# The last 64 rows of two weight matrices on low partitions, and q computed in rows, in a gated attention and MLP decode kernel

## The chip, the cores and the metric

One core of one Trainium2 chip runs the kernel. The metric is the device time of one execution in microseconds (us). Engines are named as the profile names them: PE (matrix multiply), PEld (its weight loads), DVE (vector), ACT (scalar), POOL (GpSimd), SP (the engine that issues most transfers). "SPq" and "ACTq" are the instruction streams that issue transfers. Sixteen DMA engines serve the core; a transfer issued by one instruction is split over some or all of them.

## What is computed

```python
x: [8, 1, 448]                                 # B = 8 rows, D = 448
g = sigmoid((x * gate_w).sum(-1))
# attention, 16 query heads on 8 key/value heads, the last 1024 of 4096 cached positions
q = x @ wq                                     # wq [448, 4096]
p = softmax(q . k / 16) ; o = p . v            # k, v [8, 8, 1024, 256] of the caches
a = o @ wo                                     # wo [4096, 448]
# MLP
h = gelu(layernorm(x) @ w1 + b1)               # w1 [448, 1792]
b = h @ w2 + b2                                # w2 [1792, 448]
out = g * a + (1 - g) * b
```

All inputs are bf16. Keys and values are 33.6 MB each; with the weights some 77.7 MB are read for an output of 8 x 448 numbers.

## The kernel before

**Weights and inputs.** D = 448 is 3 x 128 + 64. The first 384 rows of wq and w1 lie in `wq_sb` and `w1_sb` on 128 partitions, three rows to a partition. The last 64 rows are the tail. Before the change each tail row is cut in two halves, so that the tail also fills 128 partitions: `wq_t` [128, 2048] and `w1_t` [128, 896]. The matching parts of x and of the normalised y are spread over 128 columns with zeros between (`x_e`, `y_e`, `halves`, L263), turned by PE (L273) and copied to `xT` and `yT` (L276).

**Order of the transfers.** ACT issues x, b1 and b2 (L156 to L158). SP issues w1_sb (L159), w1_t (L162), w2 (L164), three parts of wq_sb (L167) and wq_t (L168). Then `issue_to` (L187, L148) goes through a fixed list: 32 key tiles and 32 value tiles of 1 MB, with a 448 KB part of wo (`wo_sb[g]`) after every fourth key tile; the value tile lags the key tile by five; the last value tile comes in two halves, and the last wo part is the last transfer of all. Keys and values share a pool of 12 buffers (`NKV`), and a load into a used buffer waits until PE has read it. Transfers of SP and ACT together take turns on eight completion semaphores; a transfer waits until the one that used its semaphore before has landed. So at most eight are under way.

**Start of the computation.** `mlp_up` makes 14 groups of matmuls: three with `w1_sb` (L321), one with b1 (L325), one with `w1_t` (L329). DVE and ACT do the gelu (L338 to L344). `mlp_down` (L353) multiplies with w2 on two column strips of PE, 28 matmuls of 224 columns and two for b2. Then q: 128 matmuls with a 128 x 128 block of wq as the weights and 8 columns of xT (L377), which gives q already turned; two DVE instructions scale it into `qT` (L389).

**The long loop.** There are 64 steps. A step turns half a key tile with 16 PE transposes (L407), copies the result out of PSUM (DVE, L412), multiplies the step before with qT (scores, L433) and, eleven steps later, the value half tile with the softmaxed scores (`pv`, L508). Every eight steps a head's softmax is done and its part of the output projection (`o_proj`, L533). `gate_load` and `gate` are done in the middle. PE, DVE and SP take everything in program order.

**The end.** After the last value half: `pv`, `o_scale` on DVE (L519), `o_proj` with the last wo part (L533), one DVE instruction (L577), two output transfers (L581).

Of the kernel before, what the change touches and what calls it, by code (L numbers as in the profile page):

```python
# [16 lines left out]
def kernel(  # L17
# [15 lines left out]
    nc = tc.nc  # L33
# [10 lines left out]
    NB = B  # L44
# [8 lines left out]
    DC = D // P  # L53
    DM = DC * P
    TL = D - DM
    HH = HD // 2
    assert Sq == 1 and Dh % P == 0 and W % P == 0 and F % P == 0
    FH = F // 2
    NH = NF // 2
    assert TL * 2 == P and NC * R <= 2 * P and NB % TB == 0 and 3 * 32 <= P and R <= 32 and NF % 2 == 0  # L60
    qscale = float(Dh) ** -0.5
    NU = NBU * Hkv
    NSTEP = NU * TB
# [42 lines left out]
    big.tile([P, PAD], BF16, name="pad")  # L106
    NKH = rep * NJ
    wq_sb = big.tile([P, DC, HD], BF16, name="wq_sb")
    wq_t = big.tile([P, HH], BF16, name="wq_t")
    w1_sb = big.tile([P, DC, F], BF16, name="w1_sb")  # L110
    wo_sb = [big.tile([P, NKH, D], BF16, name=f"wo_sb{g}") for g in range(Hkv)]
    w1_t = big.tile([P, FH], BF16, name="w1_t")
    w2_sb = big.tile([P, NF, D], BF16, name="w2_sb")
    x_sb = consts.tile([NB, D], BF16, name="x_sb")
    gw_sb = consts.tile([NB, D], BF16, name="gw_sb")
    b1_sb = consts.tile([1, F], BF16, name="b1_sb")
# [10 lines left out]
    xT = consts.tile([P, DC + 2, NB], BF16, name="xT")  # L127
    yT = consts.tile([P, DC + 2, NB], BF16, name="yT")
    x_e = consts.tile([NB, 2, P], BF16, name="x_e")
    y_e = consts.tile([NB, 2, P], BF16, name="y_e")  # L130
    gg = consts.tile([NB, 2], F32, name="gg")
    gg4 = consts.tile([PT, 2], F32, name="gg4")
    bvec = consts.tile([PT, DN], F32, name="bvec")
    bsum = consts.tile([PT, DN], F32, name="bsum")
    res = consts.tile([PT, DN], BF16, name="res")

# [4 lines left out]
    def load(kind, n):  # L141
# [40 lines left out]
    def issue_to(k):  # L182
        while pos[0] < len(units):
            kind, n = units[pos[0]]
            if kind == "W":
                r0 = n * NKH * P
                nc.sync.dma_start(  # L187
                    wo_sb[n][:].rearrange("p (i j) n -> p i (j n)", i=rep),
                    A_wo[r0 : r0 + NKH * P, :].rearrange(
                        "(i p j) n -> p i (j n)", i=rep, j=NJ  # L190
                    ),
                )
# [26 lines left out]
    )  # L219
    for t in diag:  # L220
        nc.gpsimd.memset(t[:], 0.0)
    nc.gpsimd.memset(x_e[:], 0.0)
    nc.gpsimd.memset(y_e[:], 0.0)
    nc.gpsimd.tensor_copy(identf[:], ident[:])
    sel = consts.tile([NB, PT], F32, name="sel")
    nc.gpsimd.tensor_copy(
        sel[:].rearrange("b (j q) -> b j q", j=CT),
        ident[0:NB, 0:CP].unsqueeze(1).to_broadcast([NB, CT, CP]),
    )


    prod = consts.tile([NB, D], F32, name="prod")
# [28 lines left out]
    def halves(dst, src):
        for h in range(2):
            nc.vector.tensor_copy(  # L263
                dst[:, h, :].rearrange("b (r h) -> b r h", h=2)[:, :, h],
                src[:, DM:D],
            )

    def transposed(dst, t, t_e):
        v = t[:, 0:DM].rearrange("b (p c) -> b c p", c=DC)
        parts = [v[:, c, :] for c in range(DC)] + [t_e[:, h, :] for h in range(2)]  # L270
        tp = ps_kt.tile([P, W], BF16, tag="ktp", name="tp")
        for c, part in enumerate(parts):
            nc.tensor.transpose(  # L273
                tp[:, c * NB : (c + 1) * NB], part, ident[0:NB, 0:NB]
            )
        nc.vector.tensor_copy(  # L276
            dst[:], tp[:, 0 : len(parts) * NB].rearrange("p (c b) -> p c b", b=NB)
        )

    halves(y_e, y_sb)  # L280
    transposed(yT, y_sb, y_e)
    halves(x_e, x_sb)
    transposed(xT, x_sb, x_e)


    def gate_load():
        src = gate_w.rearrange("(o d) -> o d", o=1)
        nc.scalar.dma_start(gw_sb[:], src.to_broadcast([NB, D]))

    def gate():  # L290
        nc.vector.tensor_tensor(prod[:], x_sb[:], gw_sb[:], op=ALU.mult)
# [13 lines left out]
        nc.vector.tensor_copy(gg4[:], A_bank[0:PT, DN : DN + 2])  # L305
        nc.vector.tensor_scalar_mul(bvec[:], bsum[:], gg4[:, 1:2])


    M = {}
# [58 lines left out]
    q_ps = ps_g.tile([P, 512], F32, tag="grp", name="q_ps")
    NQ = Hq * NJ
    for c in range(DC + 1):  # L370
        for k in range(NQ):
            if c < DC:
                w, xs = wq_sb[:, c, k * P : (k + 1) * P], xT[:, c, :]
            else:
                h, kk = divmod(k, NQ // 2)
                w, xs = wq_t[:, kk * P : (kk + 1) * P], xT[:, DC + h, :]
            nc.tensor.matmul(  # L377
                q_ps[:, k * NB : (k + 1) * NB],
                lhsT=w,
                rhs=xs,  # L380
                start=(c == 0 and k == 0),
                stop=(c == DC),
                skip_group_check=True,
            )
# [161 lines left out]
    for n in range(LAST):  # L546
# [65 lines left out]
```

## Time and profile before

| what | value |
|---|---|
| median of 3 runs | 196.84 us (196.69 to 196.88) |
| the profiled execution | 196.92 us |
| its span in the profile | 195.2 us, so 1.72 us lie outside |
| PE busy, DVE busy, ACT busy | 164.2, 113.1, 6.4 us |
| DMA read | 77.68 MB, 398 GB/s over the span |
| last wo part landed | 191.33 us |
| mean granted PE clock | 0.768 |

The page gives busy times by engine, a row of 40 slices, the DMA queues, the chain of work that ended last, and the costliest groups of instructions. The trace behind it also holds one record for each DMA packet (start, duration, bytes, queue) and one for each increment that a DMA engine made on a completion semaphore. A transfer on 16 DMA engines makes 16 such increments, one as each engine's share has landed. Queue q1 is that of SP, q10 that of ACT; q8 and q14 fetch instructions for the engines.

### The profile page before, as it was taken

To read this page: it belongs to the slowest core of one execution; us is meant where nothing else is said; L and a number is where in the kernel's file an instruction comes from. 1 tells how busy PE (TensorE), PEld (TensorE's weight loads), DVE (VectorE), ACT (ScalarE), POOL (GpSimd) and SP (SyncE) were. 2 spreads that over 40 slices of the span, in tenths; PEclk is the share of its full clock that TensorE was granted. 3 is DMA by queue.
4 is the path that set the end of the run, shared out by engine and by line. 5 is a ranking of instruction groups with operands and counts; after the bars stand their busy time and mean duration, and the time that the engine had idled before them with its cause. 6 is when DMAs were issued, how large, how long until landed. Compare 5 with 4: busy or idle time off the path is not lost.

```text
span 195.2 us, 7355 instructions
## 1 busy us (share of the span) xinstructions
PE 164.2 (84%) x3417; PEld 153.6 (79%) x3417; DVE 113.1 (58%) x255; ACT 6.4 (3%) x13; POOL 2.8 (1%) x16
## 2 busy tenths in 40 slices
PE   2677799988899796958999898988898989989752
PEld 1565799988899796957999797978897989989541
DVE  3122189996477653764559674964586646766401
ACT  5000000000000000010000000000000000000000
POOL 5000000000000000000000000000000000000000
PEclk9999889997569855585569996995599655699555
DMA  6999999999999999999999999999999999999940
GB/s 215 412 426 425 425 413 426 426 423 420 421 426 422 417 425 426 425 417 431 423 423 419 422 425 428 418 421 418 425 430 417 421 425 430 426 420 425 394 176 5
DMA packets 12769, 78.14 MB, mean 400 GB/s; under 512 B 1330, under 2 KB 3523, under 8 KB 4164
## 3 DMA queue, kind: packets, MB, share of 16 engines
q1 hardware_dynamic: 12688, 77.67, 95.4%
q8 instruction: 26, 0.43, 0.8%
q10 hardware_dynamic: 52, 0.02, 0.0%
q14 instruction: 3, 0.02, 0.0%
HBM read 77.68 MB, written 0.01 MB: 398 GB/s over the span
## 4 chain that ended last, share of the span: by engine, by line
DMA 91%; PE 6%; SPq 1%; issue 0%; DVE 0%
DMA kv<-in_A_k_cache_dram 47%; DMA kv<-in_A_v_cache_dram 19%; DMA wo_sb<-in_A_wo_dram 18%; DMA wq_sb<-in_A_wq_dram 7%; PE ktp L407 4%; PE grp L433 1%; PE A_bank L533 0%; PE grp L508 0%; SPq L167 0%; PE grp L422 0%; SPq L164 0%; DVE res L577 0%; SPq L159 0%; SPq L162 0%; SPq L148 0%
## 5 line engine op out<-in xcount | busy, mean ns | idle before, releaser
L412 DVE COPY kt<-ktp 128x1024 bf16<-128x1024 bf16 x128 | 84.4, 687 | 44.4 <-PE ktp L407 43.9
L407 PE MATMUL ktp<-ident,kv 128*128 128x128 bf16 x1024 | 89.0, 257 | 7.9 <-DMA kv<-in_A_k_cache_dram 6.7
L407 PEld LDWEIGHTS <-kv 128*128 128x128 bf16 x1024 | 78.0, 118 | 10.9 <-DMA kv<-in_A_k_cache_dram 7.9
L508 PE MATMUL grp<-e,kv 128*128 128x4 bf16 x1024 | 35.6, 166 | 2.6 <-DMA kv<-in_A_v_cache_dram 2.5
L508 PEld LDWEIGHTS <-kv 128*128 128x128 bf16 x1024 | 32.6, 101 | 5.6 <-DMA kv<-in_A_v_cache_dram 2.8
L433 PE MATMUL grp<-qT,kt 128*128 128x4 bf16 x1024 | 36.6, 166 | 0.3 <-DVE kt L412 0.2
L433 PEld LDWEIGHTS <-kt 128*128 128x128 bf16 x1024 | 34.6, 100 | 1.8 <-issue 0.6
L482 ACT ACTIVATE e<-grp 128x256 bf16<-128x256 f32 x8 | 3.1, 383 | 161.8 <-PE grp L475 161.8
L491 PE MATMUL A_bank<-zs,onesf 128*128 128x16 f32 x16 | 3.6, 299 | 4.5 <-DVE zs L487 4.5
L491 PEld LDWEIGHTS A_bank<-zs,onesf 128*128 128x128 f32 x16 | 2.8, 218 | 5.1 <-DVE zs L487 5.1
L533 PE MATMUL A_bank<-wo_sb,ot 128*8 128x224 bf16 x64 | 5.5, 305 | 0.8 <-DMA wo_sb<-in_A_wo_dram 0.5
L321 PE MATMUL h_ps<-yT,w_sb 128*128 128x8 bf16 x42 | 4.2, 195 | 1.2 <-DMA w_sb<-in_B_w_dram 1.2
L495 DVE RECIPROCAL rz<-A_bank 128x16 f32<-128x16 f32 x8 | 2.1, 258 | 5.4 <-PE A_bank L491 5.4
L519 DVE TENSOR_TENSOR ot<-grp,rz 128x32 bf16<-128x32 f32 x8 | 1.5, 186 | 6.4 <-PE grp L508 6.4
L487 DVE TENSOR_REDUCE zs<-e 128x16 f32<-128x256 bf16 x8 | 4.8, 602 | 0.0
L353 PE MATMUL b_ps<-w_sb,hT 128*8 128x224 bf16 x28 | 2.8, 388 | 2.4 <-DVE b_ps L349 2.4
L338 DVE COPY z<-h_ps 128x112 f32<-128x112 f32 x1 | 0.3, 275 | 7.7 <-PE h_ps L329 7.7
L321 PEld LDWEIGHTS <-w_sb 128*128 128x128 bf16 x42 | 3.6, 152 | 1.3 <-DMA w_sb<-in_B_w_dram 1.3
L475 PE MATMUL grp<-diag,onesb 128*128 128x256 bf16 x8 | 2.5, 308 | 2.2 <-DVE diag L469 1.9
L353 PEld LDWEIGHTS <-hT 128*8 128x8 bf16 x28 | 1.8, 121 | 3.0 <-DVE hT L344 2.2
L446 DVE TENSOR_REDUCE pm<-grp 128x16 f32<-128x256 f32 x8 | 3.3, 415 | 0.6 <-PE grp L433 0.6
L533 PEld LDWEIGHTS <-ot 128*8 128x8 bf16 x64 | 2.6, 93 | 1.3 <-issue 0.4
(82 smaller groups left out, 53.6 us busy)
## 6 DMA issues: line engine op xcount, KB each, us to landing
kv<-in_A_k_cache_dram SPq DMA_DIRECT2D x32, 1024.0 KB, 18.3
kv<-in_A_v_cache_dram SPq DMA_DIRECT2D x31, 1024.0 KB, 18.3
wo_sb<-in_A_wo_dram SPq DMA_DIRECT2D x8, 448.0 KB, 18.3
wq_sb<-in_A_wq_dram SPq DMA_DIRECT2D x3, 1024.0 KB, 12.1
w_sb<-in_B_w_dram SPq DMA_DIRECT2D x1, 1568.0 KB
w_sb<-in_B_w_dram SPq DMA_DIRECT2D x1, 1344.0 KB, 5.9
kv<-in_A_v_cache_dram SPq DMA_DIRECT2D x2, 512.0 KB, 19.8
wq_t<-in_A_wq_dram SPq DMA_DIRECT2D x1, 512.0 KB, 14.5
```

Source lines behind the costliest of these rows:

```text
L321: nc.tensor.matmul(o, lhsT=cols(w1_sb[:, c, h * FH : (h + 1) * FH]), rhs=yT[:, c, :], start=(c == 0), stop=False,)
L353: nc.tensor.matmul(b_ps[CP * j : CP * j + NB, 0:DN], lhsT=M["hT"][:, k * NB : (k + 1) * NB] if k < NF else onesb[0:1, 0:NB], rhs=w2_sb[:, ...
L407: nc.tensor.transpose(ktp[:, c * P : (c + 1) * P], K[:, h * HC + c, j * P : (j + 1) * P], ident[:],)
L412: nc.vector.tensor_copy(kt[:, j, :], ktp[:])
L433: nc.tensor.matmul(G[g][:, s : s + RU], lhsT=kt[:, j, c * P : (c + 1) * P], rhs=qT[:, j, g, bu * TB : (bu + 1) * TB, :].rearrange("p t i - ...
L446: nc.vector.reduce_max(pm[:], G[g][:, S0 : S0 + NC * R].rearrange("p (c r) -> p r c", r=R), axis=AXIS.X,)
L475: nc.tensor.matmul(G[g][:, S0 : S0 + NC * R].rearrange("p (c r) -> p c r", c=NC), lhsT=onesb[:], rhs=diag[g % 2][:].unsqueeze(1).to_broadc ...
L482: nc.scalar.activation(e[:], G[g][:, S0 : S0 + NC * R], ACT.Exp)
L487: nc.vector.reduce_sum(zs[:], E[g][:].rearrange("p (c r) -> p r c", r=R), axis=AXIS.X)
L491: nc.tensor.matmul(zc, lhsT=onesf[:], rhs=zs[:], start=False, stop=True, skip_group_check=True)
L508: nc.tensor.matmul(G[g][:, o : o + RU], lhsT=V[:, cc, :].rearrange("p (q j) -> p j q", j=NJ)[:, j, :], rhs=E[g][:, cc * R + bu * RU : cc * ...
L533: nc.tensor.matmul(A_bank[CP * j : CP * j + NB, 0:DN], lhsT=ot[:].rearrange("p j (b i) -> p j i b", i=rep)[:, h, i, :], rhs=wo_sb[g][:, k, ...
```

## The change

Four things change together.

1. **The tails.** The tail rows are no longer cut in two. Rows 0 to 47 of the tail go to partitions 0 to 23 and 32 to 55 of `wq_t` and `w1_t` by two transfers whose source has the outer dimension 6 (six groups of four rows); rows 48 to 63 go to partitions 0 to 15 of `wq_u` and `w1_u` by one transfer of outer dimension 4. A row is 8192 B for wq and 3584 B for w1. `wq_u` and `w1_u` lie in the memory of the last four wo parts. The unused partitions of `wq_t` and `w1_t` are set to zero first, by POOL and DVE. The three transfers of w1 are issued by ACT and those of wq by SP, after the POOL work; all key, value and wo loads are issued behind them.
2. **b1** is loaded as row 64 of `w1_t`, and row 64 of that part of `yT` is set to 1, so one matmul of 65 rows takes the place of the b1 matmul. The small tail part is one more matmul; there are still five in a group.
3. **q** is computed with 32 columns of xT as the weights (8 of them used) and 512 columns of wq streaming: 5 x 8 matmuls on four column strips, into two PSUM banks. DVE and ACT scale one bank each into `q_r`, PE turns it with 8 transposes, DVE makes qT of it with four copies.
4. **Memory.** gw_sb lies in w1_sb, and bvec in bsum.

On the instruction streams PE goes from 6801 to 6641 rows; SP has three transfers for the wq tail and none for the w1 tail; ACT has the three w1 transfers ahead of its first activation.

```diff
-    wq_t = big.tile([P, HH], BF16, name="wq_t")
+    wq_t = big.tile([P, HD], BF16, name="wq_t")
...
+    NHI = 4
+    wo_sb = [big.tile([P, NKH, D], BF16, name=f"wo_sb{g}") for g in range(Hkv - NHI)]
+    wo_hi = big.tile([P, NHI * NKH * D], BF16, name="wo_hi")
...
+    wq_u = wo_hi[0:T2, 0:HD]
+    w1_u = wo_hi[0:T2, HD : HD + F]
+    w1_t = big.tile([P, F], BF16, name="w1_t")
...
+    def tail(eng, dst1, dst2, w):
+        for h in range(2):
+            eng.dma_start(
+                dst1[32 * h : 32 * h + T1 // 2, :],
+                w[DM + h * T1 // 2 : DM + (h + 1) * T1 // 2, :].rearrange(
+                    "(r i) n -> i r n", i=6
+                ),
+            )
+        eng.dma_start(dst2, w[DM + T1 : D, :].rearrange("(r i) n -> i r n", i=4))
+
+    nc.vector.memset(w1_t[0:TP, :], 0.0)
     nc.scalar.dma_start(x_sb[:], xf)
-    nc.scalar.dma_start(b1_sb[:], B_b1.rearrange("(o f) -> o f", o=1))
+    nc.scalar.dma_start(w1_t[TP : TP + 1, :], B_b1.rearrange("(o f) -> o f", o=1))
...
-    nc.sync.dma_start(w1_t[:], B_w1[DM:D, :].rearrange("r (h n) -> (r h) n", h=2))
+    tail(nc.scalar, w1_t, w1_u, B_w1)
...
-    nc.sync.dma_start(wq_t[:], A_wq[DM:D, :].rearrange("r (h n) -> (r h) n", h=2))
...
-    issue_to(NKV)
...
+    nc.gpsimd.memset(wq_t[0:TP, :], 0.0)
+    tail(nc.sync, wq_t, wq_u, A_wq)
+    issue_to(NKV)
...
-                nc.tensor.matmul(
-                    o, lhsT=cols(b1_sb[:, h * FH : (h + 1) * FH]),
-                    rhs=onesb[0:1, 0:NB], start=False, stop=False,
-                )
-                nc.tensor.matmul(
-                    o, lhsT=cols(w1_t[:]), rhs=yT[:, DC + h, :],
-                    start=False, stop=True,
-                )
+                nc.tensor.matmul(
+                    o, lhsT=cols(w1_t[0 : TP + 1, h * FH : (h + 1) * FH]),
+                    rhs=yT[0 : TP + 1, DC, 0:NB], start=False, stop=False,
+                )
+                nc.tensor.matmul(
+                    o, lhsT=cols(w1_u[:, h * FH : (h + 1) * FH]),
+                    rhs=yT[0:T2, DC + 1, 0:NB], start=False, stop=True,
+                )
...
+    q_ps = [ps_g.tile([P, QW], F32, tag="grp", name="q_ps") for _ in range(NT)]
+    wq_c = [(wq_sb[:, c, :], xT[:, c, :]) for c in range(DC)]
+    wq_c += [(wq_t[0:TP, :], xT[0:TP, DC, :]), (wq_u, xT[0:T2, DC + 1, :])]
+    for c, (w, xs) in enumerate(wq_c):
+        for t in range(NT):
+            for k in range(NS):
+                n0 = QW * (NS * t + k)
+                nc.tensor.matmul(
+                    q_ps[t][CP * k : CP * (k + 1), :],
+                    lhsT=xs,
+                    rhs=w[:, n0 : n0 + QW],
+                    start=(c == 0),
+                    stop=(c == len(wq_c) - 1),
+                    tile_position=(0, CP * k),
+                    skip_group_check=True,
+                )
+    nc.vector.tensor_scalar_mul(q_r[:, 0:QW], q_ps[0][:], qscale)
+    nc.scalar.activation(q_r[:, QW : 2 * QW], q_ps[1][:], ACT.Copy, scale=qscale)
+    for t in range(NT):
+        for k in range(rep * NJ):
+            o = (t * rep * NJ + k) * P
+            nc.tensor.transpose(q_tp[:, o : o + P], q_r[:, o : o + P], ident[:])
+    for t in range(NT):
+        for i in range(rep):
+            nc.vector.tensor_copy(
+                qT[:, :, NS * t : NS * (t + 1), :, i], q_v[:, t, i, :, :, 0:NB]
+            )
```

More of the change, by code (lines that the diff above doesn't have):

```diff
@@ L55 @@
     TL = D - DM
-    HH = HD // 2
+    T1, T2, TP = 48, 16, 64
     assert Sq == 1 and Dh % P == 0 and W % P == 0 and F % P == 0
@@ L59 @@
     NH = NF // 2
-    assert TL * 2 == P and NC * R <= 2 * P and NB % TB == 0 and 3 * 32 <= P and R <= 32 and NF % 2 == 0
+    assert TL == T1 + T2 and F % P == 0 and NC * R <= 2 * P and NB % TB == 0 and 3 * 32 <= P and R <= 32 and NF % 2 == 0
     qscale = float(Dh) ** -0.5
@@ L108 @@
     wq_sb = big.tile([P, DC, HD], BF16, name="wq_sb")
-    wq_t = big.tile([P, HH], BF16, name="wq_t")
+    wq_t = big.tile([P, HD], BF16, name="wq_t")
     w1_sb = big.tile([P, DC, F], BF16, name="w1_sb")
-    wo_sb = [big.tile([P, NKH, D], BF16, name=f"wo_sb{g}") for g in range(Hkv)]
-    w1_t = big.tile([P, FH], BF16, name="w1_t")
+    NHI = 4
+    wo_sb = [big.tile([P, NKH, D], BF16, name=f"wo_sb{g}") for g in range(Hkv - NHI)]
+    wo_hi = big.tile([P, NHI * NKH * D], BF16, name="wo_hi")
+    wo_sb += [
+        wo_hi[:, k * NKH * D : (k + 1) * NKH * D].rearrange("p (k n) -> p k n", n=D)
+        for k in range(NHI)
+    ]
+    wq_u = wo_hi[0:T2, 0:HD]
+    w1_u = wo_hi[0:T2, HD : HD + F]
+    assert HD + F <= NHI * NKH * D
+    w1_t = big.tile([P, F], BF16, name="w1_t")
     w2_sb = big.tile([P, NF, D], BF16, name="w2_sb")
     x_sb = consts.tile([NB, D], BF16, name="x_sb")
-    gw_sb = consts.tile([NB, D], BF16, name="gw_sb")
-    b1_sb = consts.tile([1, F], BF16, name="b1_sb")
+    gw_sb = w1_sb[0:NB, 0, 0:D]
     b2_sb = consts.tile([1, D], BF16, name="b2_sb")
@@ L126 @@
     qT = consts.tile([P, NJ, Hkv, NB, rep], BF16, name="qT")
[L127 to L130, printed above, removed]
+    xT = consts.tile([P, DC + 2, CP], BF16, name="xT")
+    yT = consts.tile([P, DC + 2, CP], BF16, name="yT")
+    x_e = consts.tile([NB, TP + T2], BF16, name="x_e")
+    y_e = consts.tile([NB, TP + T2], BF16, name="y_e")
     gg = consts.tile([NB, 2], F32, name="gg")
     gg4 = consts.tile([PT, 2], F32, name="gg4")
-    bvec = consts.tile([PT, DN], F32, name="bvec")
     bsum = consts.tile([PT, DN], F32, name="bsum")
@@ L187, in issue_to @@
                 nc.sync.dma_start(
-                    wo_sb[n][:].rearrange("p (i j) n -> p i (j n)", i=rep),
+                    wo_sb[n][:, :, :].rearrange("p (i j) n -> p i (j n)", i=rep),
                     A_wo[r0 : r0 + NKH * P, :].rearrange(
@@ L221 @@
         nc.gpsimd.memset(t[:], 0.0)
-    nc.gpsimd.memset(x_e[:], 0.0)
-    nc.gpsimd.memset(y_e[:], 0.0)
+    for t in (x_e, y_e, xT, yT):
+        nc.gpsimd.memset(t[:], 0.0)
+    nc.gpsimd.memset(yT[TP : TP + 1, DC, :], 1.0)
     nc.gpsimd.tensor_copy(identf[:], ident[:])
@@ L259, with transposed @@
     )
[L261 to L265, printed above, removed]
-            )
[L268 to L272, printed above, removed]
+    def transposed(dst, t, t_e):
+        nc.vector.tensor_copy(
+            t_e[:, 0:TP].rearrange("b (h z) -> b h z", h=2)[:, :, 0 : T1 // 2].rearrange(
+                "b h (i r) -> b h i r", r=4
+            ),
+            t[:, DM : DM + T1].rearrange("b (h r i) -> b h i r", h=2, i=6),
+        )
+        nc.vector.tensor_copy(
+            t_e[:, TP : TP + T2].rearrange("b (i r) -> b i r", r=4),
+            t[:, DM + T1 : D].rearrange("b (r i) -> b i r", i=4),
+        )
+        v = t[:, 0:DM].rearrange("b (p c) -> b c p", c=DC)
+        tp = ps_kt.tile([P, W], BF16, tag="ktp", name="tp")
+        for c in range(DC):
+            nc.tensor.transpose(
+                tp[:, c * NB : (c + 1) * NB], v[:, c, :], ident[0:NB, 0:NB]
+            )
+        for c, (lo, n) in enumerate(((0, TP), (TP, T2))):
             nc.tensor.transpose(
-                tp[:, c * NB : (c + 1) * NB], part, ident[0:NB, 0:NB]
+                tp[0:n, (DC + c) * NB : (DC + c + 1) * NB],
+                t_e[:, lo : lo + n], ident[0:NB, 0:NB],
             )
         nc.vector.tensor_copy(
-            dst[:], tp[:, 0 : len(parts) * NB].rearrange("p (c b) -> p c b", b=NB)
+            dst[:, 0:DC, 0:NB], tp[:, 0 : DC * NB].rearrange("p (c b) -> p c b", b=NB)
         )
-    halves(y_e, y_sb)
+        for c, n in enumerate((TP, T2)):
+            nc.vector.tensor_copy(
+                dst[0:n, DC + c, 0:NB], tp[0:n, (DC + c) * NB : (DC + c + 1) * NB]
+            )
     transposed(yT, y_sb, y_e)
-    halves(x_e, x_sb)
     transposed(xT, x_sb, x_e)
@@ L287, in gate_load @@
         src = gate_w.rearrange("(o d) -> o d", o=1)
-        nc.scalar.dma_start(gw_sb[:], src.to_broadcast([NB, D]))
+        nc.scalar.dma_start(gw_sb, src.to_broadcast([NB, D]))
     def gate():
-        nc.vector.tensor_tensor(prod[:], x_sb[:], gw_sb[:], op=ALU.mult)
+        nc.vector.tensor_tensor(prod[:], x_sb[:], gw_sb, op=ALU.mult)
         nc.vector.reduce_sum(gsum[:], prod[:], axis=AXIS.X)
@@ L305, in gate @@
         nc.vector.tensor_copy(gg4[:], A_bank[0:PT, DN : DN + 2])
-        nc.vector.tensor_scalar_mul(bvec[:], bsum[:], gg4[:, 1:2])
+        nc.vector.tensor_scalar_mul(bsum[:], bsum[:], gg4[:, 1:2])
     M = {}
@@ L322, in mlp_up @@
                         o, lhsT=cols(w1_sb[:, c, h * FH : (h + 1) * FH]),
-                        rhs=yT[:, c, :], start=(c == 0), stop=False,
+                        rhs=yT[:, c, 0:NB], start=(c == 0), stop=False,
                     )
                 nc.tensor.matmul(
-                    o, lhsT=cols(b1_sb[:, h * FH : (h + 1) * FH]),
-                    rhs=onesb[0:1, 0:NB], start=False, stop=False,
+                    o, lhsT=cols(w1_t[0 : TP + 1, h * FH : (h + 1) * FH]),
+                    rhs=yT[0 : TP + 1, DC, 0:NB], start=False, stop=False,
                 )
                 nc.tensor.matmul(
-                    o, lhsT=cols(w1_t[:]), rhs=yT[:, DC + h, :],
-                    start=False, stop=True,
+                    o, lhsT=cols(w1_u[:, h * FH : (h + 1) * FH]),
+                    rhs=yT[0:T2, DC + 1, 0:NB], start=False, stop=True,
                 )
@@ L365 @@
     mlp_down()
[L368 to L376, printed above, removed]
-            nc.tensor.matmul(
[L378 to L383, printed above, removed]
-            )
@@ L385 @@
-    q_v = q_ps[:, 0 : Hq * NJ * NB].rearrange(
-        "p (g i j b) -> p i j g b", i=rep, j=NJ, b=NB
-    )
-    for i in range(rep):
-        nc.vector.tensor_scalar_mul(qT[:, :, :, :, i], q_v[:, i], qscale)
+    QW = 512
+    NS = P // CP
+    NT = HD // (NS * QW)
+    assert QW == rep * NJ * P and NT * NS == Hkv
+    q_ps = [ps_g.tile([P, QW], F32, tag="grp", name="q_ps") for _ in range(NT)]
+    wq_c = [(wq_sb[:, c, :], xT[:, c, :]) for c in range(DC)]
+    wq_c += [(wq_t[0:TP, :], xT[0:TP, DC, :]), (wq_u, xT[0:T2, DC + 1, :])]
@@ new lines @@
+    q_r = ktpool.tile([P, NJ, W], BF16, tag="kt", name="q_r")
+    q_r = q_r[:].rearrange("p j w -> p (j w)")
+    nc.vector.tensor_scalar_mul(q_r[:, 0:QW], q_ps[0][:], qscale)
+    nc.scalar.activation(q_r[:, QW : 2 * QW], q_ps[1][:], ACT.Copy, scale=qscale)
+    q_tp = ps_kt.tile([P, W], BF16, tag="ktp", name="q_tp")
+    for t in range(NT):
+        for k in range(rep * NJ):
+            o = (t * rep * NJ + k) * P
+            nc.tensor.transpose(q_tp[:, o : o + P], q_r[:, o : o + P], ident[:])
@@ L392 @@
+    q_v = q_tp[:].rearrange(
+        "p (t i j s z) -> p t i j s z", t=NT, i=rep, j=NJ, s=NS
+    )
+    for t in range(NT):
+        for i in range(rep):
+            nc.vector.tensor_copy(
+                qT[:, :, NS * t : NS * (t + 1), :, i], q_v[:, t, i, :, :, 0:NB]
+            )
     KT = {}
@@ L577 @@
     nc.vector.scalar_tensor_tensor(
-        res[:], in0=A_ps, scalar=gg4[:, 0:1], in1=bvec[:], op0=ALU.mult, op1=ALU.add
+        res[:], in0=A_ps, scalar=gg4[:, 0:1], in1=bsum[:], op0=ALU.mult, op1=ALU.add
     )
```

## The prediction, made before the changed kernel had run

> **What bounds the kernel now.** I read the slices first, then the queues, then the chain of work that ended last, and last the packet and landing records of the trace.
>
> ```profile
> PE   2677799988899796958999898988898989989752
> PEclk9999889997569855585569996995599655699555
> DMA  6999999999999999999999999999999999999940
> ...
> q1 hardware_dynamic: 12688, 77.67, 95.4%
> q8 instruction: 26, 0.43, 0.8%
> ...
> DMA 91%; PE 6%; SPq 1%; issue 0%; DVE 0%
> ```
>
> The DMA engines are full from the second slice to the 38th. PE is busy, but its granted clock falls to half in many slices and its work still gets done: it follows the loads. The chain says the same; its last pieces (start, length, what) are:
>
> ```profile
> 154.50 19.52 DMA kv<-in_A_k_cache_dram
> 174.01 0.02 issue
> 174.03 17.30 DMA wo_sb<-in_A_wo_dram
> 191.33 0.04 issue
> 191.37 0.93 PE A_bank L533 x8
> ```
>
> The last wo part was issued at 174.03 and landed at 191.33; 3.87 us later the span ends. So the end is set by the landing of the last transfer. But the DMA row falls to 4 in the slice from 185.4, five microseconds before that landing. Why? The trace has one landing per DMA engine. For the last transfer, counted from the first at 184.98 us:
>
> ```
> 0  .07  .14  .43  .49  .52  .73  1.88 | 4.65  4.71  4.72  4.74  4.80  4.91  5.67  6.35
> ```
>
> For the third part of wq_sb, at 17.48 us, the sixteen lay within 0.86. So **eight engines fall behind by over 4 us, and the kernel waits for the slowest one**. The packet records show why: each of the 26 fetches on q8 (16 KB, 0.88 to 0.97 us) lengthens the next 8 KB packet of that engine from 0.31 to about 0.8, together 1.43 us. After each fetch exactly one engine's landings jump by that much, and the jumps go round eight engines; the first of them has been hit four times by the 25th fetch (180.7) and is the 6.35. The other eight are never hit by q8. The 1.88 is an engine on which two 8 KB fetches of q14 (at 40.95 and 123.95) cost 0.84 each.
>
> **The step that matters: where the tails go.** A packet of 8192 B takes 306 ns from start to start on its engine, 4096 B 155, 1792 B 71; a row of 3584 B (b1's packet) 137. Before, each engine had 8 packets of 4096 B (wq_t) and 8 of 1792 B (w1_t): 8 x 0.155 + 8 x 0.071 = 1.81 us.
>
> In the trace a transfer has as many landings as its outer dimension allows: x and gate_w (8 rows) eight, b1 (one row) one, all others 16. So I take outer dimension 6 as six engines with four rows each, and 4 as four. If each begins at the same first engine:
> - four engines get 12 rows of each tail: 12 x 0.306 + 12 x 0.137 = 5.31, that is +3.50 us;
> - two get 8 rows: 8 x 0.306 + 8 x 0.137 = 3.54, +1.73 us;
> - ten get none: -1.81 us.
>
> Which engines are these? Packets on one engine follow each other in a fixed rhythm, so each can be followed by its phase, and q10's packets show as steps in it. gate_w's eight packets (63.3 to 63.6 us) fell on six engines that q8 never hits and on two that it hits. b1's single packet (5.09 us) was on one of the six. So the set of one lies in the set of eight, and I take the sets of four and six to nest likewise; that the six are just the never-hit ones is my choice, since the two hit ones follow each other in the round and a run of eight neighbours that leaves out the first engine would have them at the end of the eight. The trace doesn't number the engines.
>
> At the last transfer these six had 0, .07, .14, .48, about .5, and 1.88. Sum at the end: the slowest engine 6.35 - 1.81 = **4.54**; the other hit ones at most 5.67 - 1.81 = 3.86; the four at most .52 + 3.50 = 4.02; the 1.88 engine 1.88 + 1.73 = 3.61 if it is among the two, 5.38 if among the four. I take the first (b1's engine is a different one, and a uniform pick would make it 2 in 5; but if a queue's fetches go to neighbours, as I take q8's to, it is as likely in either pair; I call it four to three). The last landing moves from 191.33 to 189.52: **-1.81 us**. The profiled execution, 196.92, becomes 195.11; its median stood 0.08 below it.
>
> The Trainium skill, "DMA: Bandwidth & Descriptors", speaks against this change in "Rules for kernel authors": a small outermost dimension confines a transfer to few engines, so put a multiple of 16 there. Its section "Why a DMA increments its semaphore by 16 and not by 1" says that SP's and ACT's transfers use the lowest-numbered engines, which agrees with the nesting above. By the rule alone the four engines' 3.50 us would all be added, giving 200.4; by the landings they have 4.1 us of slack and nothing is added.
>
> **What lies beside it.**
> - The start of PE's work gets later, under cover. The w1 tail is on q10 beside q1. b1, issued at 1.43, landed at 5.96; 12 packets that alternate with w2's (235 ns) add up to 12 x (0.137 + 0.235) = 4.5. So L329's successor starts between 7 and 10.6 us instead of 7.3. ACT issues three transfers (0.23 to 0.59 each) after a DVE memset (about 1 us; 224 columns took 0.24) ahead of rstd, so yT comes 1 to 2.5 us later, inside that. Queued behind are the gelu on DVE and ACT, mlp_down, q.
> - q: 40 matmuls of 512 columns. Nearest row:
>
> ```profile
> L353 PE MATMUL b_ps<-w_sb,hT 128*8 128x224 bf16 x28 | 2.8, 388 | 2.4 <-DVE b_ps L349 2.4
> ```
>
> 28 of 224 columns on two strips in 2.78 us, 0.099 each, or 0.44 ns a column: the strips did not overlap. 40 x 512 x 0.44 = 9.0 us against 3.5 (18.73 to 22.2) now: +5.5; were four strips side by side, a quarter, 2.3: -1.2. I take 9.0, the nearer row. (The skill's "TensorEngine Tiling (Array Packing)", "Theoretical Speedup", allows up to 4 times for 32 columns, which would be the 2.3; L353 shows none of it for two.) Scaling and turning add some 1.5 (16 transposes take 1.05; a DVE instruction of 224 columns 0.38). So the first key transposes start between 23 and 34 us, now 23.54. Key tile 0 itself lands at about 25, behind the tails on the four engines.
> - What hides this: 12 buffers, and a queue in which a load waits 18 us.
>
> ```profile
> SPq L148 <- PE ktp L407: 4.4, 12, 0.6
> ```
>
> SP has waited for PE to free a buffer for 0.6 us at most, with 18.3 us of transfers queued ahead. Ten microseconds of lateness halve that queue and leave the engines fed. PE then catches up: a step with pv takes 1.7 us at full clock, two steps 3.4, while a key and a value tile take 4.9. Without this cover each microsecond beyond 18 would stall the loads.
> - SP's three wq-tail transfers wait for POOL's memset (256 columns took 0.30, so 4096 some 3 to 5 us, done by about 9), and SP's next transfers for the eight semaphores, w2's landing among them (near 12). By then wq_sb is queued to 17: hidden; if not, the same price.
> - PE has 160 rows fewer of 6801, that is 0.6 of a fetch (262 rows each): the 25th moves from 180.7 to about 184, still before its engine ends. Should it miss, the four engines' 4.02 would set the end: 194.6.
> - Memory reuse (gw_sb, bsum, wo_hi) waits only for work long done: nothing.
>
> **At the end** PE must not become late:
>
> ```profile
> 187.79 1.01 PE L508 MATMUL grp<-e,kv 128*128 128x4 bf16 x32 [1.41 <-DMA kv<-in_A_v_cache_dram]
> 189.01 0.59 PE L508 MATMUL grp<-e,kv 128*128 128x4 bf16 x16 [0.20 <-DMA kv<-in_A_v_cache_dram]
> 190.24 0.58 PE L508 MATMUL grp<-e,kv 128*128 128x4 bf16 x16 [0.64 <-DMA kv<-in_A_v_cache_dram]
> ```
>
> PE waited 1.41 + 0.20 + 0.64 = 2.25 us here for values. With values 1.81 earlier, 0.44 is left even if PE's own schedule doesn't move.
>
> **Rivals.**
> 1. The 1.88 engine is one of the four: 5.38 sets the end, -0.97: 195.9. For it: nothing numbers the engine. Against: only the pairing above.
> 2. One of the four is an engine that q8 hits: 4.65 to 4.91 before, plus 3.50, is 8.2 to 8.4, +1.8 to +2.1: **198.9, slower**. It decides as soon as one of the four was more than 6.35 - 3.50 = 2.85 behind; among the two, a hit one gives 4.65 + 1.73 = 6.4, no change. Against it: b1's engine is not hit, and six of the eight aren't.
> 3. PE is late at the end by more than the 0.44, because it caught up badly after the late start or ran its last part at half clock as it does now (0.50 after 180): the gain shrinks from 1.81 towards nothing, 195.5 to 196.8.
> 4. The change doesn't do what it says: the shares are spread evenly over all 16 (6 + 6 + 4) or begin elsewhere each time. Then all engines carry about what they did, and the time stays at 196.8.
>
> **Numbers.** Forecast (with a missed fetch) 40%, rival 1 30%, rival 3 10% (a third of it no change), rival 4 6%, rival 2 and anything like it 14%. What a measurement can tell from no change is about 0.2%, 0.4 us. Faster: 40 + 30 + 7 = 77%; same 6 + 3 = 9%; slower 14%. Range: 194.4 (missed fetch, with 0.2 to spare) to 196.9, which takes in all but rival 2; the forecast's own range is 194.6 to 195.6.
>
> **What would show it.** The landings of the last transfer should span some 4.5 us instead of 6.35, the last near 189.5; the wq tail should have 6, 6 and 4 landings. Key tile 0 should land near 25, PE's first key transposes start near 30. Wrong would be a span of landings of 8 with four engines last (rival 2), a wait of PE for nothing but itself after 185 (rival 3), or SP's waits for PE growing to many microseconds.

## The result, and the profile after

The changed kernel takes **197.81 us** (median of 6 executions, 197.10 to 198.66), the kernel before 196.84 (196.64 to 197.00, 6 executions on the same chip). The ratio is 1.0049, with a 95% interval of 1.0031 to 1.0067: it is slower by half a per cent, where 195.1 was forecast. The six executions are not one cluster: 197.10, 197.11, 197.52, 198.09, 198.54, 198.66. The profiled one took 197.11, its span is 195.4.

The page of the changed kernel, in the rows that were read before (slices, then queues with packets, MB and share, then the shares of the chain that ended last):

```profile
PEclk9999999999975556985558969997985555996655
DMA  6999999999999999999999999999999999999940
...
q1 hardware_dynamic: 12480, 77.44, 95.0%
q8 instruction: 26, 0.43, 0.8%
q10 hardware_dynamic: 132, 0.25, 0.4%
...
DMA 81%; PE 13%; POOL 3%; DVE 1%; issue 0%; POOLq 0%; SPq 0%
```

Nothing has changed in kind: the DMA row is full to slice 38 and then falls to 4, as before, and q8 still makes 26 fetches. The last pieces of the chain (start, length, what):

```profile
156.04 19.53 DMA kv<-in_A_k_cache_dram
175.59 15.88 DMA wo_hi<-in_A_wo_dram
191.50 0.93 PE A_bank L584 x8
```

The end is again the landing of the last wo part, at 191.47 where it was 191.33. Its sixteen landings, one for each DMA engine, counted from the first of them (us; this distance is called "lag" from here on):

```
before, first at 184.98:  0  .07  .14  .43  .49  .52  .73  1.88 | 4.65  4.71  4.72  4.74  4.80  4.91  5.67  6.35
after,  first at 183.36:  0  .18  .42 | 4.29  4.48  4.52  4.54  4.55  4.61  4.63 | 5.58  5.66  5.77  6.02  7.28  8.10
```

So the first landing did come 1.62 earlier, about the 1.81 that ten engines were to save. What came in its place is one engine at **8.10**: 183.36 + 8.10 = 191.46. Which one? The lags of earlier transfers tell, followed from one to the next (only the six largest are shown):

```
first landing   the six largest lags
 27.0           3.85  4.04  5.61  5.63  5.69  5.76
 38.0           4.02  5.40  5.59  5.67  5.74  6.57
 90.5           4.08  5.58  5.66  5.78  6.44  6.82
139.4           4.69* 5.62  5.70  5.81  7.27  8.23
179.7           4.62* 5.61  5.69  5.75  7.28  8.10     (* by now another engine may stand here)
```

At 27 us the six engines of the tails stand as the prediction wrote them: two near 3.9 and four near 5.7 (it had 3.54 and 5.31). Then one of the **two** jumps by about 1.4 three times: 3.86, 5.40, 6.8, 8.1, in the transfers that first land at 38, 88 and 139 us. Each time a fetch on q8 falls between its landing before and the late one: at 39.6, 92.9 and 144.5 us, the 3rd, the 11th and the 19th of the 26. They lie eight apart, as they should if the fetches go round eight engines. One of the four grows by 0.8 twice (5.76, 6.57, 7.28): that is the engine with two fetches of q14 (42.0 and 117.3 us).

On PE, at the end, the last pv matmuls (start, length, line, what, and in brackets the wait before them):

```profile
186.74 2.15 PE L559 MATMUL grp<-e,kv 128*128 128x4 bf16 x64
...
189.12 0.59 PE L559 MATMUL grp<-e,kv 128*128 128x4 bf16 x16 [0.23 <-DMA kv<-in_A_v_cache_dram]
190.39 0.59 PE L559 MATMUL grp<-e,kv 128*128 128x4 bf16 x16 [0.69 <-DMA kv<-in_A_v_cache_dram]
...
191.50 0.91 PE L584 MATMUL A_bank<-wo_hi,ot 128*8 128x224 bf16 x8 [0.53 <-DMA wo_hi<-in_A_wo_dram]
```

PE waits for values for 0.23 + 0.69 = 0.92 us, where it waited 2.25 before. It is nearer to being late in this execution, but it still waits.

At the start, the same view, before and after:

```profile
15.74 2.78 PE L353 MATMUL b_ps<-w_sb,hT 128*8 128x224 bf16 x28 [2.41 <-DVE b_ps L349]
...
23.54 2.74 PE L407 MATMUL ktp<-ident,kv 128*128 128x128 bf16 x24 [1.33 <-DMA kv<-in_A_k_cache_dram]
```

```profile
20.61 2.78 PE L388 MATMUL b_ps<-w_sb,hT 128*8 128x224 bf16 x28 [2.41 <-DVE b_ps L384]
...
23.60 2.39 PE L414 MATMUL q_ps<-wq_sb,xT 128*32 128x512 bf16 x24
25.92 0.61 PE L414 MATMUL q_ps<-wq_t,xT 64*32 64x512 bf16 x8
26.46 0.61 PE L414 MATMUL q_ps<-wo_hi,xT 16*32 16x512 bf16 x8
27.66 0.62 PE L432 MATMUL q_tp<-ident,q_r 128*128 128x128 bf16 x8 [0.58 <-DVE q_r L426]
28.11 1.95 PE L458 MATMUL ktp<-ident,kv 128*128 128x128 bf16 x32
```

mlp_down begins 4.87 us later than before (20.61 for 15.74), and the first key transposes 4.57 later (28.11 for 23.54). q itself takes 3.47 us, as before.

### The profile page after: what moved, and what is told of

It is laid out like the page before. It is cut to its first block, busy times and chain, and to the rows that moved or that the text cites. A ratio compares the mean times of both kernels' runs of the same rounds, so it can differ in the third digit from the quotient of the medians.

```text
span 195.4 us, 7217 instructions
## 1 busy us (share of the span) xinstructions
PE 163.2 (84%) x3337; PEld 150.2 (77%) x3337; DVE 115.8 (59%) x263; ACT 7.0 (4%) x14; POOL 6.5 (3%) x20
## 4 chain that ended last, share of the span: by engine, by line
DMA 81%; PE 13%; POOL 3%; DVE 1%; issue 0%; POOLq 0%; SPq 0%
DMA kv<-in_A_k_cache_dram 37%; DMA kv<-in_A_v_cache_dram 19%; DMA wo_hi<-in_A_wo_dram 18%; PE ktp L458 8%; DMA wq_t<-in_A_wq_dram 7%; PE grp L484 2%; POOL wq_t L253 2%; PE grp L559 2%; PE A_bank L584 1%; DVE w_t L177 0%; DVE kt L463 0%; POOL par L233 0%; PE A_bank L542 0%; PE grp L473 0%; DVE zs L538 0%
## 5 line engine op out<-in xcount | busy, mean ns | idle before, releaser
L458 PE MATMUL ktp<-ident,kv 128*128 128x128 bf16 x1024 | 87.1, 254 | 4.6 <-DMA kv<-in_A_k_cache_dram 4.5
L458 PEld LDWEIGHTS <-kv 128*128 128x128 bf16 x1024 | 76.3, 117 | 7.6 <-DMA kv<-in_A_k_cache_dram 5.7
L559 PEld LDWEIGHTS <-kv 128*128 128x128 bf16 x1024 | 32.6, 100 | 4.9 <-issue 2.8
L388 PE MATMUL b_ps<-w_sb,hT 128*8 128x224 bf16 x28 | 2.8, 388 | 2.4 <-DVE b_ps L384 2.4
L388 PEld LDWEIGHTS <-hT 128*8 128x8 bf16 x28 | 1.8, 121 | 3.0 <-DVE hT L379 2.2
L364 PE MATMUL h_ps<-yT,wo_hi 16*128 16x8 bf16 x14 | 2.9, 211 | 1.1 <-DMA wo_hi<-in_B_w_dram 1.1
## 6 DMA issues: line engine op xcount, KB each, us to landing
w_sb<-in_B_w_dram SPq DMA_DIRECT2D x1, 1568.0 KB, 10.6
```

What stands on the lines that cost most here:

```text
L364: nc.tensor.matmul(o, lhsT=cols(w1_u[:, h * FH : (h + 1) * FH]), rhs=yT[0:T2, DC + 1, 0:NB], start=False, stop=True,)
L388: nc.tensor.matmul(b_ps[CP * j : CP * j + NB, 0:DN], lhsT=M["hT"][:, k * NB : (k + 1) * NB] if k < NF else onesb[0:1, 0:NB], rhs=w2_sb[:, ...
L458: nc.tensor.transpose(ktp[:, c * P : (c + 1) * P], K[:, h * HC + c, j * P : (j + 1) * P], ident[:],)
L559: nc.tensor.matmul(G[g][:, o : o + RU], lhsT=V[:, cc, :].rearrange("p (q j) -> p j q", j=NJ)[:, j, :], rhs=E[g][:, cc * R + bu * RU : cc * ...
```

## The experiments

Two theories stood against each other. **Theory 1:** the end is set by one DMA engine that carries 8 rows of each tail and is also hit by q8. The trace doesn't number the engines; "the low five" are here those that a transfer of outer dimension 5 uses, and "the sixth" is the one that outer dimension 6 adds to them, if the sets nest. **Theory 2:** PE's later start costs the time.

### e1: eight extra loads, to number the engines

The kernel before, with eight small loads of outer dimension 8 down to 1 after the tail of wq:

```diff
+    for k in range(Hkv, 0, -1):
+        nc.sync.dma_start(
+            wo_sb[k - 1][0 : 4 * k, :, :].rearrange("p k n -> p (k n)"),
+            B_w1[0 : 4 * k, :].rearrange("(r i) n -> i r n", i=k),
+        )
```

> The kernel before, with eight small extra loads behind the wq loads (into wo buffers that are loaded properly later): outer dimension 8, 7, ... 1, four rows of 3584 B to an engine. So the engine counted k-th from the lowest gets (8 - k) x 4 x 0.137 = (8 - k) x 0.55 us more, k from 0, and its landings carry its number. Theory 1 (the end is set by one DMA engine that belongs to the two with outer dimension 6 but not 4, and that the fetches on q8 also hit): among the numbers 0 to 5 exactly one engine, 4 or 5, shows the jumps of 1.43 us, and none of 0 to 3 does. Theory 2 (the later and longer start of PE's work costs the time, the tails' engines don't matter): none of 0 to 5 is hit. Time about 196.8 to 198 either way.

Measured: 200.13 us in one execution (span 198.4). The lags that were to be read can't be read in it. Its slices say why:

```profile
DMA  5999799999999999999999999999999999999940
GB/s 207 412 435 374 290 420 413 433 421 414 423 429 423 415 424 429 425 425 416 431 421 421 413 430 428 420 411 427 428 428 417 422 431 421 421 425 425 413 194 5
```

In the fifth slice the DMA row falls to 7 and the rate to 290 GB/s. The eight small loads took the eight completion semaphores on which the transfers take turns. SP was busy issuing them from 7.03 to 19.86 us, with waits for landings between, and issued the first key tile at 20.11, where it was 7.07 before. So the engines ran dry, and the lags to be read were wiped out. The last landing came at 188.68 + 5.84 = 194.52, that is 3.19 later, for 0.52 MB more. The run says nothing on the two theories; it shows that a row of short transfers starved the engines here.

### e2: q in rows, alone

Part 3 of the change put into the kernel before; the tails, b1 and the order of the transfers stay. The edit is that of the change at L403 to L440, with `wq_t` and its halves as they were.

> The kernel before with part 3 of the change alone: q in rows on four column strips, tails loaded as before on all 16 engines. Theory 1: the end is that of before, 196.6 to 197.1, with a spread of some 0.3 us. Theory 2: most of the loss and of the spread is here, 197.3 to 198.7.

Measured: 196.72 us (196.36 to 196.92, 12 executions) beside 196.78; ratio 0.9989 (0.9979 to 0.9999). Part 3 alone costs nothing. Its start on PE:

```profile
18.57 1.77 PE L384 MATMUL q_ps<-wq_sb,xT 128*32 128x512 bf16 x24
20.18 0.60 PE L384 MATMUL q_ps<-wq_t,xT 128*32 128x512 bf16 x8
21.36 0.62 PE L402 MATMUL q_tp<-ident,q_r 128*128 128x128 bf16 x8 [0.59 <-DVE q_r L396]
23.44 1.96 PE L428 MATMUL ktp<-ident,kv 128*128 128x128 bf16 x32 [1.45 <-DMA kv<-in_A_k_cache_dram]
```

32 matmuls of 512 columns take 2.21 us, 0.069 each; at L353's rate they would take 0.225 each, 7.2 in all. So the four strips do overlap, by a factor of 3.3.

### e3: the tails without q in rows

The changed kernel with q computed as before (weights are the 128-column blocks of wq), so parts 1, 2 and 4 without 3:

```diff
-                nc.tensor.matmul(
-                    q_ps[t][CP * k : CP * (k + 1), :],
-                    lhsT=xs,
-                    rhs=w[:, n0 : n0 + QW],
...
+            nc.tensor.matmul(
+                q_ps[:, k * NB : (k + 1) * NB],
+                lhsT=w,
+                rhs=xs,
```

> The changed kernel with q computed as before (128-column blocks of wq as weights): parts 1, 2 and 4 of the change alone, tails on four and six engines. Theory 1: as the changed kernel, median 197.1 to 198.6, with single runs from 197 to 198.7. Theory 2: near before, 196.6 to 197.1.

Measured: 197.32 us (196.87 to 198.60, 12 executions), ratio 1.0041 (1.0020 to 1.0062). So the loss is not with q in rows. Seven executions lie at 196.87 to 197.39 and five at 198.16 to 198.60. The profiled one is of the second kind (198.38), and its last transfer shows what makes it so:

```
e3, first at 183.37:  0 .21 .27 | 4.23 4.29 4.34 4.34 4.41 4.50 4.51 | 5.43 5.62 5.63 5.83 7.07 9.37
```

One engine's lag rises four times there, the last time from 7.9 to 9.6, in the transfer that first lands at 179.7 us. The fetches (27 in this kernel) go round eight engines, so some engines get three and some four, and the place of the sixth engine in the round differs between executions: it took the 3rd, 11th and 19th fetch in the profile above, and the 2nd, 10th, 18th and 26th (at 187.3 us) in this one. With three it ends at 8.10, with four at 9.37. The two clusters, about 197.0 and 198.4, are one fetch apart.

### e4: the changed kernel again

> The changed kernel once more, for its spread and for a second profile. Theory 1 holds that the runs differ because 26 fetches go round eight engines, so that the round begins at another engine in each execution and the late engine gets three fetches or four: single runs near 197.1 and near 198.5, and in the profile the last engine's lag over the first is 3.85 + n x 1.43 us with n = 3 (8.1) or 4 (9.6) or between if the last fetch comes late. Theory 2: the last transfer's landings span the same 8.1 us in slow and fast executions, and a slow one shows PE waiting for itself at the end.

Measured: 197.04 us (196.89 to 198.59, 12 executions), ratio 1.0015 (1.0001 to 1.0030). Eleven executions lie at 196.89 to 197.23, one at 198.59. In the profiled one (197.10) the last engine lands 8.03 after the first, at 191.47. It again had three fetches, but other ones: the 8th, 16th and 24th. So the round does begin elsewhere in two executions of one kernel. The 1.0049 of the first comparison is then a mixture: with three fetches on the sixth engine the change costs about 0.15%, with four about 0.9%. The four were seen in e3; of the changed kernel itself no execution above 198 was profiled.

PE's end in this profile:

```profile
187.98 1.01 PE L559 MATMUL grp<-e,kv 128*128 128x4 bf16 x32 [1.43 <-DMA kv<-in_A_v_cache_dram]
189.20 0.59 PE L559 MATMUL grp<-e,kv 128*128 128x4 bf16 x16 [0.21 <-DMA kv<-in_A_v_cache_dram]
190.41 0.59 PE L559 MATMUL grp<-e,kv 128*128 128x4 bf16 x16 [0.62 <-DMA kv<-in_A_v_cache_dram]
```

It waits for values for 2.26 us, as long as before the change, and the end comes no earlier for it.

### e5: the sixth engine left free

The kernel of e2, with the wq tail on five engines: three transfers of 20 rows with outer dimension 5 and one of 4 rows with outer dimension 4. `w1_t` stays as it was before the change, on sixteen engines.

```diff
+    NHI = 5
...
+    SETS = [(0, 0, 20, 5), (0, 32, 20, 5), (1, 0, 20, 5), (1, 32, 4, 4)]
...
+    nc.gpsimd.memset(wo_hi[0:TP, 0 : 2 * HD], 0.0)
+    off = DM
+    for tl, base, rows, i in SETS:
+        nc.sync.dma_start(
+            wq_r[tl][base : base + rows, :],
+            A_wq[off : off + rows, :].rearrange("(r i) n -> i r n", i=i),
+        )
+        off += rows
+    issue_to(NKV)
```

> The kernel before with q in rows, and of the tails only that of wq on few engines: three transfers of 20 rows with outer dimension 5 and one of 4 rows with 4; the w1 tail stays on 16 engines. The lowest four engines get 13 rows x 0.306 - 1.24 = +2.74 us, the fifth +2.43, the others -1.24. Theory 1, if the hit engine of the two is the sixth (left out here): the slowest engine is a hit one with 6.35 - 1.24 = 5.11, the end moves by -1.2, 195.6. Theory 1, if it is the fifth: 4.7 + 2.43 = 7.1 with three fetches or 8.6 with four, +0.8 to +2.2, 197.6 to 199. Theory 2 (late start of PE): as the changed kernel, 197.1 to 198.6.

Measured: **196.09 us** (195.95 to 196.24, 5 executions), ratio 0.9967 (0.9955 to 0.9979). It is faster than both kernels, by less than expected. The lags of its last transfer:

```
e5, first at 183.80:  0 .36 .66 4.00 4.24 4.26 4.56 4.57 4.62 4.65 4.70 4.83 4.96 5.00 6.46 6.52
```

At 27.6 us the five had 3.64 to 4.83, and until the end none of them jumps by the 1.4 of a q8 fetch. One grows by 0.9 twice (at about 41 and 115 us, as q14's engine did above) and ends at 6.46, another by 0.6 once, after q14's third fetch at 105.0. The largest of the others is 6.52. The two are level, so moving more rows should gain nothing: 183.80 + 6.52 = 190.32, 1.01 earlier than before. The time gained less: in this kernel 2.0 us lie outside the span (196.20 less 194.2), where it was 1.7 before, and the same holds for all executions of e5, e6, e8 and e9 (1.9 to 2.2). What this added time is, the profile doesn't show. PE waits for this landing and has time (same columns as above):

```profile
186.83 1.01 PE L556 MATMUL grp<-e,kv 128*128 128x4 bf16 x32 [1.46 <-DMA kv<-in_A_v_cache_dram]
188.05 0.58 PE L556 MATMUL grp<-e,kv 128*128 128x4 bf16 x16 [0.20 <-DMA kv<-in_A_v_cache_dram]
189.28 0.58 PE L556 MATMUL grp<-e,kv 128*128 128x4 bf16 x16 [0.65 <-DMA kv<-in_A_v_cache_dram]
...
190.36 0.91 PE L581 MATMUL A_bank<-wo_hi,ot 128*8 128x224 bf16 x8 [0.50 <-DMA wo_hi<-in_A_wo_dram]
```

### e6: four engines and a transfer on sixteen

The kernel of e5 with another split:

```diff
-    SETS = [(0, 0, 20, 5), (0, 32, 20, 5), (1, 0, 20, 5), (1, 32, 4, 4)]
+    SETS = [(0, 0, 16, 4), (0, 32, 16, 4), (1, 0, 16, 4), (1, 32, 16, 16)]
```

> As the run with five engines, but three transfers of 16 rows with outer dimension 4 and one of 16 rows with 16: the lowest four engines get 13 rows, +2.74 us, all others one, 0.306 - 1.24 = -0.93. Theory 1: no hit engine is among the four; the hit ones end at 6.35 - 0.93 = 5.42, the engine with q14's fetches at 1.88 + 2.74 = 4.6: the end moves by -0.9 to 195.9, single runs within some 0.4 us. Theory 2: 197.1 to 198.6.

Measured: 198.02 us (197.59 to 199.68, 6 executions), ratio 1.0075 (1.0046 to 1.0104). This miss is large. In the profiled execution (199.37, one of the two slowest of the six) the lags end at 6.34, no more than before, but the first landing is at 185.32, 1.52 later than in e5. The transfers lost this at the start: the fourth slice moves 341 GB/s, and key tile 0 first lands at 21.51 us where e5 has 20.09. The last wo part landed at 185.32 + 6.34 = 191.66, and the kernel did not even wait for it:

```profile
PEclk9999999999979998566559999655699755555855
...
GB/s 211 415 433 341 402 410 432 424 422 414 425 430 422 415 422 425 429 415 429 422 427 417 425 424 424 419 417 426 427 425 419 423 422 427 424 425 426 367 140 5
```

```profile
190.46 2.70 PE L556 MATMUL grp<-e,kv 128*128 128x4 bf16 x96
...
193.44 0.91 PE L581 MATMUL A_bank<-wo_hi,ot 128*8 128x224 bf16 x8 [0.28 <-DVE ot L567]
```

All of the last 96 pv matmuls run without a wait, and o_proj waits for DVE, not for the transfer: here PE was late, with a granted clock of 0.50 from 160 to 180 us (0.93 in e5, 0.78 in the changed kernel). That is rival 3, in another kernel. The executions near 197.8 were not profiled, so whether PE was late in them too is open.

### e7: eight fetches fewer

The kernel before without its 1024 score matmuls (L433), which leaves out the scores, so that q8 makes 18 fetches:

```diff
-                nc.tensor.matmul(
-                    G[g][:, s : s + RU],
-                    lhsT=kt[:, j, c * P : (c + 1) * P],
...
```

> The kernel before without the 1024 score matmuls and their weight loads (the scores stay what the mask alone gives), so 2048 instructions, eight fetches of 256, are left out. Theory 1: each hit engine has one fetch fewer, the landings of the last transfer span 6.35 - 1.43 = 4.9 us, 195.4. A theory in which PE's own work sets the end: more than that is gained, since 18 us of PE work go; one in which neither fetches nor PE matter: 196.8.

Measured: 195.44 us (195.30 to 195.94, 4 executions), ratio 0.9938 (0.9925 to 0.9951).

```profile
q8 instruction: 18, 0.29, 0.5%
```

The lags of the last transfer are 0 to 0.57 on seven engines, 1.74 (q14), 2.78 to 3.46 on six and 4.78 and 4.85 on two: two fetches or three, where before it was three or four. The last landing is at 189.89, 1.44 earlier: one fetch. Every byte of the loads is still moved. PE has less to do as well, but it was not what the end waited for before, and no more was gained than one fetch. So the fetches of the instruction stream do set the end, as read from the packets.

### e8: from five to six

The kernel of e5, its wq tail split as in the changed kernel (six and four engines):

```diff
-    SETS = [(0, 0, 20, 5), (0, 32, 20, 5), (1, 0, 20, 5), (1, 32, 4, 4)]
+    SETS = [(0, 0, 24, 6), (0, 32, 24, 6), (1, 0, 16, 4)]
```

> The kernel of e5 with one size changed: the wq tail has the split of the changed kernel (24, 24 and 16 rows by outer dimension 6, 6 and 4) in place of 20, 20, 20 rows by 5 and 4 by 4; the w1 tail stays on sixteen engines and q stays in rows. The lowest four engines carry 12 packets of 8192 B (they had 12 or 13), the fifth 8 (12), and the sixth 8 where it had none. Theory 1 (the sixth engine is one that q8 hits): its lag grows by 8 x 0.306 = 2.45. With three fetches it ends at 2.45 + 3 x 1.43 = 6.7 behind the first, with four at 8.2, plus up to 0.5 of its own place, in place of 6.52: the last landing near 190.5 to 191 or near 192 to 192.5, so 196.3 to 196.8 in one kind of execution and 197.8 to 198.2 in the other, and the landings of the first key tiles show two engines near 2.5 and four near 3.7, of which one of the two jumps by 1.4 later on. If the sixth engine isn't hit: every low engine carries the same or less than in e5, 196.1 or below.

Measured: 196.68 us (196.34 to 198.32, 12 executions) beside 196.74; ratio 0.9996 (0.9979 to 1.0014). At 27 us two engines are at 2.60 and 2.80 and four at 3.80 to 3.97; the one at 2.80 is then 4.35 (38 us), 5.73 (91 us), 7.16 (140 us) and ends at 7.00, the last of all: 183.66 + 7.00 = 190.66. This is the sixth engine, with three fetches, and the last landing is 0.34 later than in e5. One execution in twelve is at 198.32, as by a fourth fetch. The median gain of e5 is gone, but e9 shows that this can't be put down to the sixth engine alone.

### e9: all on four

The kernel of e5 with four transfers of 16 rows, each of outer dimension 4, so e6 without its transfer on sixteen engines:

```diff
-    SETS = [(0, 0, 20, 5), (0, 32, 20, 5), (1, 0, 20, 5), (1, 32, 4, 4)]
+    SETS = [(0, 0, 16, 4), (0, 32, 16, 4), (1, 0, 16, 4), (1, 32, 16, 4)]
```

> The kernel of e5 with the wq tail by four transfers of 16 rows, each of outer dimension 4; so e6 without its fourth transfer on sixteen engines. The lowest four engines carry 16 packets of 8192 B, 4.90, that is 3.66 more than before (in the changed kernel it is 3.50 more), and the fifth and the sixth nothing. Theory 1, with nothing else: at the end the four are at 4.9 to 5.4 behind the first landing, the one with two fetches of q14 at 6.5, the hit ones at most 6.5, so the last landing is near 190.3 and the time 196.1, as in e5. If it was the backlog on four engines that let the others run dry in e6 (key tile 0 first landed at 21.51 there, 20.09 in e5): key tile 0 is late again, by 1 us or more, and the time is 197 or above. If it was e6's fourth transfer, key tile 0 lands near 19.8.

Measured: 196.64 us (196.32 to 197.58, 12 executions), ratio 0.9997 (0.9983 to 1.0011). Key tile 0 first lands at 20.03, so the backlog on four engines does not starve the others, though it is longer than in e6. e6 differs from this run by one transfer alone, its sixteen single rows behind three transfers that go to four engines, so its late key tile 0 comes with that one; why it held up the free engines by more than a microsecond was not settled. Three of the four end at 4.91 to 5.10 and the fourth, hit twice by q14, at 6.78, the last: 183.76 + 6.78 = 190.54. As in e5 the last landing is about a microsecond earlier than before; the profiled execution took 196.43, two took 197.57 and 197.58, and none of the longer ones was profiled. So the median gain of e5 was not repeated here, though the sixth engine is free.

## Why the prediction was wrong, point by point

**The bound was right.** The landing of the last transfer on its slowest engine sets the end, before and after, and e7 moved it by one fetch (1.44 measured, 1.43 read from the packets).

**The shares were right.** Two engines at 3.85 and 4.04 and four at 5.61 to 5.76 at 27 us, for 3.54 and 5.31; the wq tail had 6, 6 and 4 landings; key tile 0 landed last at 25.41 for "about 25"; the ten free engines were 1.62 earlier for 1.81.

**The step that failed** is "that the six are just the never-hit ones is my choice". The low five were never hit by q8, the sixth was. e5 (none of the five is hit), e8 (with a sixth, one of the two is) and the changed kernel agree. So the slowest engine was not a hit one relieved of its rows (4.54 in the prediction) but a hit one with 8 rows of each tail on top. Its sum is then 8 x 0.306 + 8 x 0.137 + 3 x 1.43 = 7.83, and 8.10 was measured. The prediction had this sum, as an aside to rival 2: "among the two, a hit one gives 4.65 + 1.73 = 6.4, no change". From the old first landing, 191.46 is 6.48. So the case was priced, and rightly so far; what it lacked is the fourth fetch, which makes it 1.4 us worse in those executions in which the round begins so that this engine gets one. With it the median is slower and not unchanged. The evidence was too thin for the choice: gate_w's eight engines had shown that two of the low eight are hit, and b1's single packet spoke for one engine, not for six. The order of the hits was then read so that it fitted. Before the change it hardly mattered where the round begins: 26 fetches on eight engines give four to two of them in any case, and the six executions lay within 0.36 us. After it, it matters whether the sixth is one of these.

**Rival 1 was right as well**, behind it: the 1.88 engine is one of the four. It ends at 183.36 + 7.28 = 190.64, where 5.38 after 184.98 is 190.36. With the sixth engine free, the time would still have been about 196.2 (an estimate, from 190.64 in place of 191.33), not 195.1.

**Rival 3 was nearer than thought.** The cover of 0.44 us assumed that PE's own schedule didn't move. In the first profile it did; the zs matmuls at the end, before and after:

```profile
184.93 0.59 PE L491 MATMUL A_bank<-zs,onesf 128*128 128x16 f32 x2
186.31 0.59 PE L542 MATMUL A_bank<-zs,onesf 128*128 128x16 f32 x2
```

If the values had come 1.81 earlier, PE would have had 96 matmuls from 186.74 on; at e6's 2.70 for 96 they end at 189.44, and o_proj starts some 0.28 later, at 189.72, for a landing at 189.52. That is an estimate; e6 shows the case itself. In e4, the same kernel, these matmuls ran at 184.92, so this differs between executions and was not shown to come from the change.

**The start.** The tail of w1 held up L329's successor (L364) to 12.14, not "between 7 and 10.6": it waited for `w1_t` (1.28) and then for `w1_u` (1.11). The turning of y ahead of it was later too, at 7.84 where it was 4.24, for "1 to 2.5": the DVE instruction that makes y_sb took 1.65 us, 0.38 before, while POOL's memset of `wq_t` ran (4.16 to 7.66); whether that is the cause was not tested. q was put at 9.0 us by L353's rate and took 3.47; 2.3 would have been the other end. By 0.225 a matmul at L353's rate, 0.087 here is 2.6 times as fast and 0.069 in e2 is 3.3 times. The Trainium skill, "TensorEngine Tiling (Array Packing)", "Theoretical Speedup", allows up to 4 times for 32 columns. The two errors nearly cancelled, which was luck: 28.11 for "near 30". Neither cost anything: SP's longest wait for PE stayed at half a microsecond (total us, times, longest):

```profile
SPq L158 <- PE ktp L458: 3.6, 9, 0.5
```

Theory 2 falls by this, by e4 (PE waits for values at the end as long as before), by e2 (q in rows, no loss) and by e3 (the loss without q in rows).

**The rule against small outer dimensions.** The Trainium skill, "DMA: Bandwidth & Descriptors", "Rules for kernel authors", asks for a multiple of 16 outermost. Taken alone, the prediction reckoned, it would have all the 3.50 added. The measured cost is neither that nor a gain for every small dimension: 5 on one tail gave 0.33% (e5), 6 (e8) and 4 (e9) gave nothing in the median, 6 and 4 on both tails cost 0.15% to 0.9%.

**What stays open:** why the executions at 197.52 and 198.09 lie between the two clusters (a fourth fetch that comes late might do it, the 26th falls at 189.1 us, but neither was profiled); the held-up engines of e6; the longer executions of e9, and with them why only e5 gained in the median; the added time outside the span.

## What to carry to other kernels

When a loop is bound by transfers, look at the landings of the last one engine by engine: a mean of full engines hides that some were hit by instruction fetches and that the end waits for the slowest. Work can be moved to the free engines by a small outer dimension, but first find out which engines those are, by a load of that very dimension whose lags are followed through a run. Here one hit engine among six turned the forecast gain of 1.81 us into a last landing 0.14 later with three fetches and, in e3, 1.40 later with four. Count instructions too: 8 fetches fewer gave 0.62% (e7, which leaves out the scores), more than any placement of the tails.

## What the runs showed of the hardware

- An engine that falls behind by one fetch (1.43 us) or by a tail (3.5 to 5.3) kept that lag to the end: the lags of the key tiles moved by less than 0.2 us in 100 us where no fetch fell.
- The round of the fetches does not begin at the same engine in every execution (the sixth took the 3rd, 11th and 19th in the first profile of the changed kernel, the 8th, 16th and 24th in e4). So 26 on eight engines put three or four on a given one, and e3's two clusters lie 1.4 us apart.
- Four column strips of 32 columns with 512 streamed columns overlapped: 0.069 to 0.087 us a matmul. With two strips, the matmuls of 224 columns at L353 and L388 took 0.099 each.
- Eight short transfers in a row (e1) made the last landing 3.2 us later. One of sixteen single rows behind three narrow ones (e6) held back key tile 0 by 1.5 us, while 64 rows on four engines (e9) did not; both are from one profile each.
